# Causal convolution on sixteen 32x32 tiles, one pool of eight PSUM banks, and a first batch on the whole array

## The chip, the cores and the metric

The kernel runs on one core of one Trainium2 chip. The metric is the device time of one execution in microseconds (us). The median of 3 runs before the change was 392.44 us (391.48 to 392.64). The profile's span, from the first to the last instruction, is about 2 us shorter than the time.

A note on words. PE is the matmul engine, DVE the vector engine, ACT the scalar engine, POOL and SP two small engines that here mostly start DMAs. PSUM is the memory that matmuls write, in 8 banks. A *batch* is one of 8 inputs, a *token tile* is 128 tokens, a *group* is 8 token tiles, and each group runs in two *phases*.

## The reference, cut to what matters

```python
def _attn_ref(x, weight):                 # x (8, 4224, 192), weight (8 heads, 7 taps)
    w = softmax(weight, axis=-1)          # (cut: written out, with 1e-9 in the sum)
    x_pad = np.concatenate([zeros(B, 6, D), x], axis=1)
    # per head of 24 channels: out[s] = sum over k of w[h, k] * x_pad[s + k]
    out = np.einsum('hk,bskhg->bshg', w, x_unf)
    return out.reshape(B, S, D)

def _moe_ref(x, U, V, w_ch1, w_ch2):      # U (4224, 32), V (32, 4224), w_ch1 (192, 768), w_ch2 (768, 192)
    xt = x.transpose(0, 2, 1)
    h = xt @ U @ V                        # mixes all tokens of a batch through rank 32
    u = x + h.transpose(0, 2, 1)
    return u + np.maximum(u @ w_ch1, 0.0) @ w_ch2
```

A batch is 4224 tokens, or 33 token tiles. Call the convolution's output y. The mixer needs U times all of a batch's y before the first h of that batch can be made. All 8 batches make 264 token tiles, or 33 groups.

## The kernel before

The convolution along tokens is a matmul with a *band matrix*. The matrix has 128x128 entries per head, with seven diagonals that hold the taps. Tokens lie on the partitions. The first six outputs of a token tile also need the last six tokens of the tile before, which a second matmul with a small corner matrix (`bandp`) adds. For batches 1 to 7, a head takes two such corner matmuls, on 64 rows each, and two full ones with 408 columns. A second copy of x, `xh`, lets one of the corner matmuls run on the other half of the rows.

```python
    un_ps = ...tile_pool(name="un_ps", bufs=6, space=PSUM)   # everything but the output sums
    ch_ps = ...tile_pool(name="ch_ps", bufs=2, space=PSUM)   # W2's sums

    def load_x(b):                         # one large DMA, after a wait for y of the batch before
        if b > 1:
            nc.gpsimd.tensor_copy(out=seen[0:1], in_=y_tiles[b - 1][0:1, 0, 0:1])
        nc.gpsimd.dma_start(out=x_tiles[b][:, 1 : 1 + NT, :], in_=x[b].rearrange("(j p) d -> p j d", p=P))
        load_xh(b)                         # (cut: x_tiles and xh_tiles of batch b are those of b - 2)

    def conv_unit(b, parts, engs, halo=True):      # parts: (first tile, end tile, head)
        def half():                        # corner matmuls, on 64 rows
            st["ps"] = [bank() for _ in parts]
            for i, (a, e, h) in enumerate(parts):
                k = i if halo else 1
                src = x_tiles[b] if k else xh_tiles[b]
                rows = slice(k * C2, (k + 1) * C2)
                nc.tensor.matmul(out=st["ps"][i][:, 0 : (e - a) * GS], lhsT=bandp[rows, h, :],
                                 rhs=src[rows, a:e, h * GS : (h + 1) * GS], start=True, stop=False)
        def full():                        # the band itself, then a copy to y
            for i, (a, e, h) in enumerate(parts):
                nc.tensor.matmul(out=st["ps"][i][...], lhsT=band[:, h, :],
                                 rhs=x_tiles[b][:, a + 1 : e + 1, h * GS : (h + 1) * GS], start=False, stop=True)
                copy(engs[i], y_tiles[b][:, a:e, h * GS : (h + 1) * GS], ...)

    def tt_unit(b):                        # U times y, 33 matmuls in turn on 4 column tiles
        ...                                # then ACT swaps two halves and DVE adds them

    def h_unit(g, half_no):                # h of 4 tiles: V on two 64-row tiles; u = y + h on DVE
        ...

    def transpose(g):                      # a DMA transposes u of one group, from the SP queue
        nc.sync.dma_start_transpose(out=uT_tiles[g]..., in_=u_ring[...])

    # w1_piece: 6 matmuls of 512 columns (W1 times uT), then Relu on ACT or DVE
    # w2_piece: matmuls of 192 columns (Relu's output times W2), + u on DVE, DMA of the output

    # head: batch 0 in 3 chunks; U transposed by DVE; W1, W2 and x of batch 1 loaded behind x of batch 0
    ...
    for g in range(NG + 1):
        for k in range(2):
            # 3 W1 pieces of group g; h of group g + 2 (k = 1) and convolution of the next batch;
            # the DMA transpose of group g + 2 (k = 1); half the W2 matmuls of group g - 1
            ...
```

PE's program order is fixed. The W1 matmuls of a group wait for that group's DMA transpose, and the transpose waits for u, which DVE makes from h.

## Time and profile before

| what | value | view |
|---|---|---|
| time, median | 392.44 us | runs |
| first W1 matmul | 42.47 us | timeline |
| PE busy after that | 337.6 of 349.6 us | stage table |
| a group without convolution | 8.76 us | chain of waits |
| a group with three heads of it | 11.3 us | chain of waits |

The first lines of the page are the busy time of each engine, its share of the span and its number of instructions. The line PEclk holds one digit for each of 40 equal slices: the clock that PE was granted, in tenths, where 9 stands for 90% or more.

```profile
PE 354.3 (90%) x3582; PEld 226.0 (58%) x3582; DVE 264.0 (67%) x481; ACT 204.0 (52%) x381; POOL 25.1 (6%) x36
...
PEclk9999999999999999999999999999999999999999
```

The stage table of before, from 42.4 us to the end, has the busy time of each engine with its instructions, the granted clock, the DMA engines' busy share and GB/s:

```profile
core 0: us, PE busy (x) PEld busy (x) DVE busy (x) ACT busy (x) POOL busy (x), PEclk, DMA share, GB/s
42.40:392.00 349.60, 337.58 (x3475) 217.34 (x3475) 243.52 (x432) 187.45 (x357) 16.27 (x18) 1.00 0.75 140
```

PE is busy for 97% of this stage. So a matmul that is taken away shortens the run, and little else does.

The chain of waits of before shows what ended last, followed back. Its columns are start, duration, engine, tile and line, and the number of instructions. L333 is W1, L354 is W2, L295 is h, L238 and L249 are the convolution's corner and full matmuls.

```profile
306.28 0.50 PE un L295 x8
...
306.81 0.60 ACT rl_4402 L342
...
307.45 0.33 PE un L238
307.78 0.45 PE un L249 x2
...
312.26 0.52 PE un L238 x4
312.78 0.80 PE un L249 x4
...
317.60 0.50 PE un L295 x8
...
337.94 0.49 PE un L295 x8
...
346.70 0.49 PE un L295 x8
```

Read from one h to the next: 317.60 - 306.28 = 11.3 us with three heads of convolution, and 346.70 - 337.94 = 8.76 us with none. Two heads in one phase cost 0.52 + 0.80 = 1.3 us. A single head costs 0.78 us plus a wait of about 0.65 us for a Relu on ACT, which has to empty a PSUM bank first.

The head, as the timeline of before shows it (start, duration, engine, line, operation, tiles; in brackets the engine's idle time before and what ended it):

```profile
23.61 4.65 DVE L388 STREAM_TRANSPOSE U_sb<-U_in 128x1024 bf16<-128x1024 bf16 x1
...
32.20 1.62 PE L269 MATMUL un<-y_sb,U_sb 128*32 128x192 bf16 x33
...
42.47 5.54 PE L333 MATMUL un<-uT,W_sb 64*128 64x512 bf16 x36 [5.45 <-DMA uT<-u_ring]
```

The U sum can't start before 32.20 us, because DVE first spends 4.65 us on transposing U, and the convolution's last chunk waits behind it. PE then waits 5.45 us for the first DMA transpose. PE's longest wait for a transpose in this kernel is that first one, as the list of PE's waits says (total, times, longest):

```profile
PE un L333 <- DMA uT<-u_ring: 5.5, 1, 5.5
```

### The profile page before, as it was taken

The numbers are of one execution on the slowest core, as the hardware profiler recorded it, in microseconds if no ns is written. First come the engines' busy times: TensorE is split into PE (matmuls) and PEld (weight loads), VectorE is DVE, ScalarE is ACT, GpSimd is POOL, SyncE is SP. The second block draws the span as 40 slices with busy tenths as digits, with TensorE's granted clock in tenths as the row PEclk, the third lists the DMA queues.
The fourth block names the chain that finished last, engine by engine and source line by source line (L and its number), as shares of the span: only waits on it lengthen the run. The fifth ranks groups of instructions, "written<-read, shape, count | busy, mean of one in ns | idle before, by whom it ended". The sixth has DMA issues, their size and how long they took to land. (4 is left out here: it accounts for less than half of the span.)

```text
span 392.1 us, 8704 instructions
## 1 busy us (share of the span) xinstructions
PE 354.3 (90%) x3582; PEld 226.0 (58%) x3582; DVE 264.0 (67%) x481; ACT 204.0 (52%) x381; POOL 25.1 (6%) x36
## 2 busy tenths in 40 slices
PE   1546699999999999999999999999999999999995
PEld 1213356655666556666565666656666566676664
DVE  4375465867677666866777667766686767888863
ACT  5325476465555655556545565555546555544450
POOL 4040020020001100020002000020000000000000
PEclk9999999999999999999999999999999999999999
DMA  7979589759927994599635996499544542655533
GB/s 183 260 113 186 77 110 183 165 115 208 172 84 145 171 221 108 139 127 195 176 97 130 197 163 115 122 172 212 134 123 102 108 118 72 146 159 129 142 100 123
DMA packets 127208, 56.89 MB, mean 145 GB/s; under 512 B 88512, under 2 KB 126912, under 8 KB 127040
## 3 DMA queue, kind: packets, MB, share of 16 engines
q1 hardware_dynamic: 92208, 43.03, 48.3%
q0 software_dynamic: 34960, 13.31, 29.0%
q8 instruction: 28, 0.46, 0.5%
q14 instruction: 12, 0.10, 0.1%
HBM read 29.86 MB, written 25.95 MB: 142 GB/s over the span
## 5 line engine op out<-in xcount | busy, mean ns | idle before, releaser
L333 PE MATMUL un<-uT,W_sb 64*128 64x512 bf16 x1188 | 141.0, 380 | 5.5 <-DMA uT<-u_ring 5.5
L364 DVE TENSOR_TENSOR o<-ch,u_ring 128x384 f32<-128x384 f32 x132 | 73.2, 557 | 74.0 <-PE ch L354 73.7
L333 PEld LDWEIGHTS <-W_sb 64*128 64x128 bf16 x1188 | 53.3, 95 | 71.7 <-issue 17.8
L67 ACT ACTIVATE y_sb<-un 128x408 bf16<-128x408 f32 (+2 forms) x124 | 54.2, 501 | 31.2 <-PE un L249 27.2
L306 DVE TENSOR_TENSOR u_ring<-y_sb,un 128x384 bf16<-128x384 bf16 (+1 forms) x136 | 64.4, 537 | 3.2 <-PE un L295 0.6
L238 PEld LDWEIGHTS <-bandp 64*128 64x128 bf16 x136 | 11.2, 99 | 28.9 <-issue 22.5
L238 PE MATMUL un<-x_sb_121,bandp 64*128 64x408 bf16 (+2 forms) x48 | 14.2, 372 | 12.7 <-DVE x_sb_121 L69 5.7
L249 PEld LDWEIGHTS <-band 128*128 128x128 bf16 x136 | 10.2, 103 | 25.5 <-issue 22.4
L295 PE MATMUL un<-tt_sb,V_sb 64*128 64x192 bf16 x264 | 22.1, 249 | 1.3 <-DVE tt_sb L281 1.1
L295 PEld LDWEIGHTS <-V_sb 64*128 64x128 bf16 x264 | 15.5, 95 | 11.3 <-issue 2.1
L249 PE MATMUL un<-x_sb_121,band 128*128 128x408 bf16 (+2 forms) x72 | 17.8, 367 | 0.0
L249 PE MATMUL un<-x_sb_125,band 128*128 128x408 bf16 x64 | 15.0, 340 | 0.0
L100 POOL CAST seen<-y_sb 1x1 f32<-1x1 bf16 x6 | 1.1, 178 | 210.9 <-ACT y_sb L67 210.9
L238 PE MATMUL un<-x_sb_125,bandp 64*128 64x408 bf16 x32 | 10.6, 331 | 1.7 <-ACT rl_445 L342 0.2
L238 PE MATMUL un<-xh_126,bandp 64*128 64x408 bf16 x32 | 9.5, 331 | 2.3 <-ACT rl_444 L342 0.4
L69 DVE CAST y_sb<-un 128x288 bf16<-128x288 f32 (+1 forms) x12 | 5.1, 433 | 9.1 <-PE un L249 9.0
L281 DVE TENSOR_TENSOR tt_sb<-un,sw 128x192 bf16<-128x192 f32 x8 | 2.9, 358 | 8.7 <-ACT sw L279 8.7
L238 PE MATMUL un<-xh_122,bandp 64*128 64x408 bf16 x24 | 7.1, 330 | 1.8 <-ACT rl_1152 L342 0.2
L186 PE MATMUL un<-taps,sel 112*128 112x128 bf16 x10 | 1.2, 309 | 7.7 <-DVE taps L177 7.7
L269 PE MATMUL un<-y_sb,U_sb 128*32 128x192 bf16 x264 | 8.0, 262 | 0.0
L342 ACT ACTIVATE rl_355<-un 128x512 bf16<-128x512 f32 x6 | 3.6, 597 | 7.6 <-PE un L333 7.4
L101 POOL DMA_DIRECT2D x_sb_125<-in_x_dram x4 | 7.3, 1821 | 1.4 <-PE ch L354 1.4
(284 smaller groups left out, 602.7 us busy)
## 6 DMA issues: line engine op xcount, KB each, us to landing
out_dram<-o SPq DMA_DIRECT2D x132, 192.0 KB, 2.6
x_sb_125<-in_x_dram POOLq DMA_DIRECT2D x4, 1584.0 KB, 17.5
x_sb_121<-in_x_dram POOLq DMA_DIRECT2D x3, 1584.0 KB, 17.5
xf<-in_x_dram SPq DMA_DIRECT2D x2, 1152.0 KB, 13.0
xf<-in_x_dram SPq DMA_DIRECT2D x1, 864.0 KB, 19.7
W_sb<-in_moe_w_ch_dram POOLq DMA_DIRECT2D x3, 288.0 KB, 5.4
V_sb<-V_sb SPq DMA_DIRECT2D x3, 264.0 KB, 8.4
uT<-u_ring SPq DMA_TRANSPOSE x33, 3.7
```

Source lines behind the costliest of these rows:

```text
L67: nc.scalar.activation(out=out_ap, in_=in_ap, func=ACT.Copy)
L69: nc.vector.tensor_copy(out=out_ap, in_=in_ap)
L101: nc.gpsimd.dma_start(out=x_tiles[b][:, 1 : 1 + NT, :], in_=x[b].rearrange("(j p) d -> p j d", p=P))
L238: nc.tensor.matmul(out=st["ps"][i][:, 0 : (e - a) * GS], lhsT=bandp[rows, h, :], rhs=src[rows, a:e, h * GS : (h + 1) * GS], start=True, st ...
L249: nc.tensor.matmul(out=ps[:, 0 : (e - a) * GS], lhsT=band[:, h, :], rhs=x_tiles[b][:, a + 1 : e + 1, h * GS : (h + 1) * GS], start=False, ...
L269: nc.tensor.matmul(out=ps[q * R : (q + 1) * R, 0:D], lhsT=U_sb[:, j, :], rhs=y_tiles[b][:, j, :], start=j < 4, stop=j >= NT - 4,)
L281: nc.vector.tensor_tensor(out=tt_tiles[b][:], in0=ps[:, 0:D], in1=sw[:], op=ALU.add)
L295: nc.tensor.matmul(out=ps[i][:, k * D : (k + 1) * D], lhsT=V_sb[rows, j * P : (j + 1) * P], rhs=tt_tiles[b][rows, :], start=True, stop=True,)
L306: nc.vector.tensor_tensor(out=u_of(t0 + 2 * i + k, n), in0=in3(y_tiles[b][:, j : j + n, :]), in1=in3(ps[i][:, k * D : (k + n) * D].rearran ...
L333: nc.tensor.matmul(out=h1[a][:], lhsT=W1_sb[rows, c, ms], rhs=uT[rows, :, c, :], start=c == 0, stop=c == 2,)
L342: nc.scalar.activation(out=rl[a][:, m, :], in_=h1[a][:], func=ACT.Relu)
L364: nc.vector.tensor_tensor(out=in3(o[:]), in0=in3(ch[g][:]), in1=u_of(t0, 2), op=ALU.add)
```

## The change

The intent is to give PE fewer and cheaper convolution matmuls, to remove the waits for PSUM banks, and to start the steady state earlier.

- Batches 1 to 7: x is stored as four row quarters of 32 partitions. Blocks of 32 tokens make the band matrix 32x32, so a pair of heads takes 64 matmuls on the 16 tiles of the array, in 4 rounds. The corner matrix is just another 32x32 block, and `xh` goes.
- One rotating pool of 8 PSUM banks instead of 6 + 2.
- h on four 32-row tiles. The U sum's four partial sums are added by one matmul with a constant matrix (`add4`) that also copies the sum to all four row blocks.
- Batch 0 stays on the whole array, in 4 chunks. U is transposed on PE. V is asked for later (at 14.3 us instead of 4.2), the weights behind the third of the four chunks (at 19.6 us instead of 22.9), the U sum follows each chunk, and the first transpose of u is done on PE. Dummy matmuls (`keep_warm`) are put in the head.

```diff
-    un_ps = ...tile_pool(name="un_ps", bufs=6, space=PSUM)
-    ch_ps = ...tile_pool(name="ch_ps", bufs=2, space=PSUM)
+    banks = ...tile_pool(name="banks", bufs=8, space=PSUM)
...
     def load_x(b):
         if b > 1:
             nc.gpsimd.tensor_copy(out=seen[0:1], in_=y_tiles[b - 1][0:1, 0, 0:1])
-        nc.gpsimd.dma_start(
-            out=x_tiles[b][:, 1 : 1 + NT, :], in_=x[b].rearrange("(j p) d -> p j d", p=P)
-        )
-        load_xh(b)
+        for r in range(4):
+            n = 4 * n_of(r, NX)
+            nc.gpsimd.dma_start(
+                out=x_bufs[b % 2][32 * r : 32 * r + 32, 1 : 1 + n, :], in_=tokens(b, r, 0, n)
+            )
+        load_before(b)                     # three small DMAs of six rows
...
+    def conv_unit(b, heads):
+        ps = [bank() for _ in range(4)]
+        for i, h in enumerate(heads):      # two heads
+            for k in range(2):             # block itself, block before
+                for r in range(4):         # row tile
+                    for c in range(4):     # column tile
+                        o = ps[r][32 * c : 32 * c + 32, 0 : e * nh * GS]
+                        nc.tensor.matmul(
+                            out=o.rearrange(...)[:, :, i * GS : (i + 1) * GS],
+                            lhsT=band_of(r, h, k),            # 32 x 32
+                            rhs=x_bufs[b % 2][rows, c + 1 - k : 4 * e + c - 2 - k : 4, h * GS : (h + 1) * GS],
+                            start=k == 0, stop=k == 1,
+                        )
+        # four copies on ACT, one for each row tile's bank
...
+    def tt_sum(b, eng):
+        nc.tensor.matmul(out=ps[:, 0:D], lhsT=add4[:], rhs=tt_tiles[b][:], start=True, stop=True)
...
+    work = {2: [(1, 0)], 3: [(1, 1)], 4: [(1, 2), (1, 3)]}     # phase: (batch, unit)
...
+            for i, (b, u) in enumerate(work.get(p, [])):
+                conv_unit(b, [2 * u, 2 * u + 1])
+                if u == 0 and b + 1 < B:
+                    load_x(b + 1)
             if k and g + 2 < NG:
-                units = [h_unit(g + 2, 0), h_unit(g + 2, 1)] + units
+                h_unit(g + 2)
+                transpose(g + 2)
```

## The prediction

> **What bounds the kernel now.** TensorE: in the stage table PE is busy 337.6 of the 349.6 us after 42.4 us, DVE 243.5, ACT 187.5. The chain of waits is almost all PE, with a few waits of 0.6 us for an ACT Relu that frees a PSUM bank.
>
> Sums read from that chain and the timeline:
> - A group of 8 token tiles without convolution takes 8.76 us (two W1 pieces of 2.05, two W2 pieces of about 2.09, h 0.50): 33 x 8.76 = 289 us.
> - A group with 3 heads of convolution takes 11.3 us. A single head in an odd phase waits about 0.65 us for a bank. Per batch 6.8 us, plus 0.95 for the U sum (33 matmuls in 0.85): 7 x 7.75 = 54 us.
> - Head: the first W1 matmul starts at 42.47 us. Batch 0's x has landed at 22.4, but a DVE transpose of U (4.65 us, until 28.3) delays the last cast, the U sum starts at 32.2, and PE waits 5.45 us for the first DMA transpose. Tail about 5 us.
>
> **What the change does, costed.**
> 1. Convolution of batches 1 to 7: per pair of heads 64 matmuls of 32x32 with 192 or 216 columns, in 4 rounds of 16 tiles. If tiles overlap fully, a round takes about 92 ns (the U sum, on 4 column tiles, starts four matmuls within 8 ns and the next four 82 ns later, for 192 columns): 0.37 us a unit. If PE can't issue faster than the 20.3 ns per load+matmul pair that this trace shows, 1.3 us. The Trainium skill (TensorE: Matmul & The Clock Gate, Part 3) gives 10.6x for 16 tiles. I take 0.75 us plus 0.15 for changing the tiling: 28 x 0.9 = 25 us, instead of 47.
> 2. With 8 rotating banks I find no bank wait over 0.3 us; the 0.65 us waits go (counted in 1).
> 3. h on four row tiles: 0.50 to about 0.30 us: -6 us.
> 4. The U sum gains an fp32 128x128 matmul and two ACT copies: about +0.5 us each, +3 us.
> 5. Head: U transposed on PE, x in four chunks, V and weights later, U sum by chunk, first transpose on PE: first W1 at about 27.5 us, -15. Given back: group 1's DMA transpose (about 1 us) and batch 1's x (about 12 us of packets after the weights, landing about 36.5, needed about 35): +2.5.
>
> ACT and DVE work is nearly unchanged (DVE about 7.7 us per group, so close to binding in groups without convolution).
>
> **Sum.** 27.5 + 2.5 + 33 x 8.56 + 25 + 10 + 5 = about 353 us; I say 354, 80% range 341 to 371. Nearly all of it is on the critical path, since PE is. Faster by over 2%: 94%; within 2%: 4%; slower: 2%.
>
> **What would show it.** First W1 near 27.5 us in the timeline; a convolution unit of 64 matmuls spanning 0.5 to 1.3 us; h 0.3 us; groups with one unit about 9.5 us, without 8.55; no Relu waits before convolution; about 1650 more PE matmuls.
>
> **What would make it wrong.** PE issue slower than 20 ns per pair (unit 1.6 to 2 us: convolution gains nothing, total about 380); the four copies per unit arriving together on ACT and holding Relus and so banks; DVE becoming the limit (groups over 9 us); batch 1's x landing past 42 us and stalling PE, whose program order puts that convolution first; slow weight loads on small tiles; the head's ACT and DVE work longer than I added up.

## More of the kernel before

A transpose is issued about one group ahead of its use.

The view of the tile uT, which holds the transposes' results, ends with the time from issue to landing:

```profile
DMA to landing us min/median/max: 3.6/3.7/9.9
```

So some transposes of before landed after 8 to 10 us instead of 3.7. Nobody on PE waited for them.

## The result, and the profile after

The changed kernel took 369.88 us (median of 4 runs, 368.55 to 371.23) against 392.54 us beside it. The result is correct. The ratio is 0.943, with a 95% interval of 0.939 to 0.947. A ratio here is the mean time of one kernel's fast runs over that of the other's in the same rounds, so it is not quite the ratio of the medians.

The page of after, the same lines:

```profile
PE 342.8 (93%) x5248; PEld 223.8 (61%) x5250; DVE 253.2 (69%) x474; ACT 197.9 (54%) x382; POOL 40.1 (11%) x72
...
PEclk9577898999899999999999999999999999999999
```

There are 1666 more matmuls, and PE is still busy less. The clock line now dips in the head, and again in slices 7 and 11, which are about 55 to 64 us and 92 to 101 us.

The stage table of after, from its first W1 matmul:

```profile
core 0: us, PE busy (x) PEld busy (x) DVE busy (x) ACT busy (x) POOL busy (x), PEclk, DMA share, GB/s
36.10:366.00 329.90, 316.83 (x5057) 209.20 (x5056) 238.35 (x429) 185.16 (x357) 29.44 (x49) 0.98 0.80 151
```

The chain of waits of after. L377 is W1, L398 W2, L328 h, L263 the convolution:

```profile
170.50 0.28 PE bank L328 x8
...
174.91 0.73 PE bank L263 x55
175.64 2.09 PE bank L398 x24
177.72 2.05 PE bank L377 x18
179.77 0.28 PE bank L328 x8
...
190.35 0.31 PE bank L328 x8
...
192.63 10.18 DMA uT<-u_ring
...
202.85 2.12 PE bank L377 x18
204.97 0.72 PE bank L263 x55
...
306.64 0.28 PE bank L328 x8
...
315.19 0.28 PE bank L328 x8
```

A group with two heads takes 179.77 - 170.50 = 9.27 us, and a unit of convolution 0.73 us. Groups without convolution take 315.19 - 306.64 = 8.55 us. No Relu stands in these groups any more. Four of 0.4 us or more are left in the chain: three on ACT before W2 matmuls near 50 and 99.5 us, and one on DVE before a convolution unit at 125.4 us, just behind a late transpose. In their place is something that before did not have: a DMA transpose that takes 10.18 us, and that W1 waits for. The list of PE's waits has six of them, and one wait of 2.1 us for no semaphore at all:

```profile
PE bank L377 <- DMA uT<-u_ring: 7.9, 6, 2.8
...
PE bank L398 <- issue: 2.1, 1, 2.1
```

The timeline of after shows the first W1 matmul, both stalls, and what stood beside them:

```profile
36.12 5.57 PE L377 MATMUL bank<-uT,W_sb 64*128 64x512 bf16 x36
...
57.22 0.34 PE L398 MATMUL bank<-W_sb,rl_533 128*128 128x192 bf16 x2
59.68 0.64 PE L398 MATMUL bank<-W_sb,rl_533 128*128 128x192 bf16 x3 [2.13 <-issue]
...
186.14 3.18 POOL L111 DMA_DIRECT2D x_sb_85<-in_x_dram  x4 [0.39 <-PE bank L398]
...
192.63 3.34 SPq L349 DMA_TRANSPOSE uT<-u_ring  x1
...
202.85 1.47 PE L377 MATMUL bank<-uT,W_sb 64*128 64x512 bf16 x12 [0.87 <-DMA uT<-u_ring]
```

The load of a batch's x is issued at 186.14 us and its last part lands at 202.63 us, by its records. The transpose issued in between, at 192.63 us, lands at 202.81 us. The last line of the tile uT's view:

```profile
DMA to landing us min/median/max: 3.6/4.1/12.2
```

An account of the span, which fell by 24.6 us (392.1 to 367.5). The first W1 matmul came 6.35 us earlier. PE's busy time after it fell by 20.8 us. PE's idle time after it, the tail after the last matmul included, rose by 2.5 us (12.1 to 14.6). In before no idle stretch after the first W1 matmul was longer than 0.3 us by PE's records. In after there are seven, of 10.0 us together. They are 1.1 us at 42.0, 2.1 at 57.6, 2.9 at 87.5, and four of 0.8 to 1.2 us, about one for each load of x.

Two readings needed tests. Is the gain really that of the tiles, or of the pool? And what took back what the forecast had promised?

### The profile page after: what moved, and what is told of

It is laid out like the page before. It is cut to its first block, busy times and chain, and to the rows that moved or that the text cites. A ratio compares the mean times of both kernels' runs of the same rounds, so it can differ in the third digit from the quotient of the medians.

```text
span 367.5 us, 12088 instructions
## 1 busy us (share of the span) xinstructions
PE 342.8 (93%) x5248; PEld 223.8 (61%) x5250; DVE 253.2 (69%) x474; ACT 197.9 (54%) x382; POOL 40.1 (11%) x72
## 4 chain that ended last, share of the span: by engine, by line
PE 73%; DMA 19%; DVE 3%; issue 2%; ACT 2%; DVEq 0%
PE bank L377 30%; PE bank L398 29%; DMA uT<-u_ring 16%; PE bank L263 4%; DMA xf<-in_x_dram 3%; PE bank L287 2%; DVE u_ring L339 2%; PE bank L328 2%; PE bank L300 2%; PE bank L316 1%; PE bank L425 1%; ACT x_sb_85 L65 1%; PE bank L360 1%; DVE y_sb L67 0%; ACT y_sb L65 0%
## 5 line engine op out<-in xcount | busy, mean ns | idle before, releaser
L377 PE MATMUL bank<-uT,W_sb 64*128 64x512 bf16 x1188 | 142.7, 384 | 8.0 <-DMA uT<-u_ring 7.9
L408 DVE TENSOR_TENSOR o<-bank,u_ring 128x384 f32<-128x384 f32 x132 | 70.8, 553 | 68.4 <-PE bank L398 58.5
L377 PEld LDWEIGHTS <-W_sb 64*128 64x128 bf16 x1188 | 53.7, 95 | 76.1 <-issue 13.5
L339 DVE TENSOR_TENSOR u_ring<-y_sb,bank 128x384 bf16<-128x384 bf16 (+1 forms) x136 | 64.5, 537 | 11.1 <-PE bank L328 11.1
L65 ACT ACTIVATE y_sb<-bank 128x432 bf16<-128x432 f32 (+5 forms) x122 | 51.3, 502 | 8.3 <-PE bank L287 6.5
L263 PEld LDWEIGHTS <-band 32*32 32x32 bf16 x1568 | 15.6, 88 | 13.3 <-issue 11.9
L328 PE MATMUL bank<-tt_sb,V_sb 32*128 32x192 bf16 x264 | 12.4, 252 | 0.9 <-ACT tt_sb L65 0.4
L328 PEld LDWEIGHTS <-V_sb 32*128 32x128 bf16 x264 | 4.3, 93 | 14.2 <-issue 13.9
L111 POOL DMA_DIRECT2D x_sb_86<-in_x_dram x16 | 12.6, 797 | 1.7 <-PE bank L398 1.4
L263 PE MATMUL bank<-x_sb_86,band 32*32 32x192 bf16 (+1 forms) x896 | 12.4, 251 | 0.1
L204 PE MATMUL bank<-warm 128*128 128x512 bf16 x23 | 8.9, 523 | 1.3 <-DVE warm L139 1.2
L111 POOL DMA_DIRECT2D x_sb_85<-in_x_dram x12 | 9.5, 802 | 1.3 <-PE bank L398 1.0
L263 PE MATMUL bank<-x_sb_85,band 32*32 32x192 bf16 (+1 forms) x672 | 9.1, 251 | 0.0
L287 PE MATMUL bank<-x_sb_85,bandp 128*128 128x288 bf16 (+3 forms) x32 | 8.8, 321 | 0.0
L263 PE MATMUL bank<-x_sb_86,bandp 32*32 32x192 bf16 x128 | 8.5, 244 | 0.0
```

The costliest lines, as they stand in the source:

```text
L65: nc.scalar.activation(out=out_ap, in_=in_ap, func=ACT.Copy)
L111: nc.gpsimd.dma_start(out=x_bufs[b % 2][32 * r : 32 * r + 32, 1 : 1 + n, :], in_=tokens(b, r, 0, n))
L204: nc.tensor.matmul(out=ps[:], lhsT=warm[:, 0:P], rhs=warm[:], start=True, stop=True)
L263: nc.tensor.matmul(out=o.rearrange("p (t g) -> p t g", g=nh * GS)[:, :, i * GS : (i + 1) * GS], lhsT=band_of(r, h, k), rhs=x_bufs[b % 2][r ...
L287: nc.tensor.matmul(out=ps[:, :, (h - i) * GS : (h - i + 1) * GS], lhsT=(bandp if k else band)[:, h, :], rhs=x_bufs[0][:, a + 1 - k : e + 1 ...
L328: nc.tensor.matmul(out=ps[r][:, k * D : (k + 1) * D], lhsT=V_sb[rows, j * P : (j + 1) * P], rhs=tt_tiles[b][rows, :], start=True, stop=True,)
```

## The experiments

Theory A: the tiles and the pool each shorten PE's work. What was given back is the contention of the x loads with the DMA transposes, and a head bound by DMA. Rivals: the tiles are worth little and the pool everything; PE stalls come from issuing or from bank waits; the head is bound by the slow clock.

The experiments ran on three chips. The kernel before ran beside each of them, with medians of 392.2 to 393.3 us, so about 1 us of a difference between runs on two chips can be the chip's. Each ratio is to before in the same rounds.

### e1: convolution on the whole array again

All else is as in after. A pair of heads takes 8 matmuls of 128 rows in place of 64 small ones, and x is loaded by one DMA.

```diff
-        for r in range(4):                 # four quarter loads and load_before
-            ...
+        nc.gpsimd.dma_start(out=x_bufs[b % 2][:, 1 : 1 + NT, :], in_=x[b].rearrange("(j p) d -> p j d", p=P))
...
+        for h in heads:
+            for a, e in ((0, 17), (17, NT)):
+                ps = bank()[:, 0 : (e - a) * GS]
+                for k in range(2):
+                    nc.tensor.matmul(..., lhsT=(bandp if k else band)[:, h, :],
+                        rhs=x_bufs[b % 2][:, a + 1 - k : e + 1 - k, ...], start=k == 0, stop=k == 1)
```

> Undoes the small tiles alone: batches 1 to 7 convolve on the whole array as batch 0 does (8 matmuls of 408 columns per pair of heads, x loaded in the old layout). Theory (the tiles save PE time): a unit takes about 1.38 us instead of 0.73, a group with one unit 9.9 us instead of 9.27, so 28 x 0.65 = +18 us of PE work over the changed kernel; part is given back because longer groups leave the DMA transposes more slack (up to 8 us of waits in the trace) and fewer instructions run short (up to 4 us): +6 to +18 us, about 376 to 388. Rival (the gain of the change is the bank pool and the head, the tiles are worth nothing): within 2 us of 369.9.

Measured: 380.46 us (378.67 to 380.65), ratio 0.968 (0.963 to 0.973), correct. So without the tiles the kernel is 10.6 us slower. Its chain of waits around one unit:

```profile
287.10 0.28 PE bank L318 x8
...
291.51 1.45 PE bank L255 x8
292.96 1.98 PE bank L388 x24
...
296.99 0.28 PE bank L318 x8
```

L318 is h in this kernel. The unit takes 1.45 us instead of 0.73, and the W2 matmuls behind it show 0.11 us less. Whole groups say it best, from one h to the next: 296.99 - 287.10 = 9.89 us against 9.27. That is 0.62 us for each of 28 units, or 17 us (an estimate from these two group times). The total moved by only 10.6 us. In the tiled kernel some 7 us of that were paid elsewhere: e1's first W1 came 0.9 us earlier (35.2), its PE gaps over 0.3 us sum to 8.4 us against 10.0, and it has neither of the two stretches of half clock that after has behind its long gaps (3.4 us long each, so about 3.4 us of delay together, an estimate). 17.4 - 0.9 - 1.6 - 3.4 = 11.5 us, close to what the total shows. The rival (tiles worth nothing) is refuted.

### e2: x of batches 2 to 7 never loaded

This kernel is wrong on purpose (relative error 1.15): the buffers keep old data. It asks what the loads cost.

```diff
-                if u == 0 and b + 1 < B:
+                if u == 0 and b + 1 < 2:
                     load_x(b + 1)
```

> Wrong result on purpose: x of batches 2 to 7 is never loaded, the convolutions read what the buffers hold. All else is the same. Theory (the waits before W1 come from DMA transposes that are queued beside the load of the next batch's x): the transposes at 78, 113, 153, 193 and 232 us land in 3.7 to 5 us instead of 10 to 12, the PE gaps of 3.1, 1.45, 1.3, 1.1 and 1.1 us before W1 go, and the slow clock window at 90 us with them: 8 to 10 us faster, about 360 to 362. Rival (those waits come from the DVE adds or from banks, which feed the transposes late): less than 2 us faster, gaps stay.

Measured: 357.28 us (355.51 to 357.46), ratio 0.909 (0.904 to 0.914). It is 12.6 us faster than after. The last line of the tile uT's view in e2:

```profile
DMA to landing us min/median/max: 3.6/3.7/5.0
```

Every transpose lands in time, and after 44 us no PE gap is over 0.5 us. The 2.1 us gap at 57 us is gone as well, though two units of convolution stand in the same phase as in after. So the loads cost about 12 us, more than I had expected, and nearly all that PE lost in after's steady state goes with them. The amount of arithmetic is the same.

### e3: the whole load of x, later

If the trouble is that the load is issued just before a transpose, issue it just after one.

```diff
-                    load_x(b + 1)                   # in the phase of the batch's first unit
+                    pending.append(b + 1)           # batches 3 to 7
...
                 transpose(g + 2)
+                if pending:                         # waits for u of the group just transposed
+                    load_x(pending.pop(), gate=u_of(t - 1, 2)[0:1, 1, 0, 0:1])
```

> The same loads, but x of batches 3 to 7 is asked for when the input of the next transpose is written, about 6 us later, so that this transpose goes ahead of the load. Theory (a transpose that is issued while a load is under way lands only when the load is through, about 17 us after the load's issue; what matters is the place of the load between two transposes): transposes take at most 8 us, no PE gap over 0.5 us before W1 from group 7 on, 6 to 10 us faster than 369.9. Rival (the DMA engines' total load is the limit, wherever the load stands): the waits move to the next transpose, within 2 us.

Measured: 374.35 us (372.11 to 376.72), ratio 0.954 (0.947 to 0.960), correct. This is a miss. It is 4.5 us slower than after, not faster. PE's waits in e3:

```profile
PE bank L380 <- DMA uT<-u_ring: 10.6, 6, 2.8
```

The waits moved to the next transpose, and grew. In this kernel the load takes 20 to 22 us from its issue to its last landing, and transposes come every 9.3 us. Wherever a load of this size starts, a transpose falls into it. The rival for this run was right that the waits move. Its size was not: it said within 2 us, and its cause, the total load of the DMA engines wherever it stands, does not fit e6, which moves the same bytes and is faster.

### e4: one unit of convolution for each phase in batch 1

This tests whether the stall at 57 us comes from the two units (128 small matmuls) in one phase.

```diff
-    work = {2: [(1, 0)], 3: [(1, 1)], 4: [(1, 2), (1, 3)]}
+    work = {1: [(1, 0)], 2: [(1, 1)], 3: [(1, 2)], 4: [(1, 3)]}
```

> The four convolution units of batch 1 stand one to a phase (1, 2, 3, 4) instead of two in phase 4. Theory (256 convolution instructions in a row outrun the fetch of PE's instructions: the 2.4 us gap at 57.3 us is in the middle of an accumulation, without a semaphore, and a 16 KB instruction fetch starts at that moment; the half clock window after it costs up to 1.7 us more): the gap goes, 2 to 5 us faster than 369.9. Rival (the gap is a chance of one profile, or the work only moves): within 1 us.

Measured: 369.73 us (366.01 to 372.15), ratio 0.939 (0.930 to 0.947), correct; the profiled run, the longest of the four, was slow. The total did not move, so as a saving it is a miss. In its profile the stall did not go. It moved to 53 us, into a unit of convolution, and is 1.5 us long there, with no semaphore; since that run was slow, this is an indication and not a size. In after, PE fetches instructions in blocks of 16 KB, and the record of one begins at 57.27 us, 0.05 us after the last matmul before the stall started. PE has 41 such fetches in after and 28 in before. (That these fetches are PE's is read from their number alone.) With e2, where no load stood beside it and the stall was absent, this points to an instruction fetch that is delayed by a load of x. The pointer is weak: the record of that fetch ends at 58.2 us, 1.5 us before PE goes on, and in e3 the same stall (57.53 to 60.17 us) begins 0.2 us before the nearest fetch. No run isolates it.

### e5: pools of 6 and 2 banks again

```diff
-    banks = ...tile_pool(name="banks", bufs=8, space=PSUM)
+    banks = ...tile_pool(name="banks", bufs=6, space=PSUM)
+    ch_ps = ...tile_pool(name="ch_ps", bufs=2, space=PSUM)
```

> Undoes the bank pool alone: 6 rotating banks and 2 for the W2 sums, as in the kernel before; the tiles stay. Theory A (the common pool is what removed the Relu waits): a convolution unit needs 4 banks right after W1 has used 6, so it waits for the Relus of the middle W1 piece, and h likewise; about 0.3 to 0.6 us for each of 28 units and 31 h, +10 us or more. Theory B (the waits went because the convolution now stands only in even phases, away from h, with one unit in a group): within 3 us of the changed kernel's 369.9.

Measured: 378.88 us (378.37 to 380.40), ratio 0.964 (0.961 to 0.967), correct. It is 9 us slower, so the pool is worth about as much as the tiles. That is Theory A, a little under its 10 us. Its chain of waits:

```profile
290.53 0.86 PE bank L264 x53
...
295.53 0.48 PE bank L329 x8
```

Here h takes 0.48 us, about as in before, although it stands on four row tiles. The convolution unit takes 0.86 us. So without the pool the row tiles gain nothing for h; I had credited the gain to them. The cause is in the start times of h's matmuls. In after, the first four start within 0.01 us. In e5, at 295.46 us, the third starts 0.10 us after the first and the fourth 0.23 us after it, each 0.05 us behind the end of a Relu (on ACT at 295.51, on DVE at 295.64) that empties the bank it needs. An earlier matmul still runs meanwhile, so PE is not idle and the list of waits shows nothing. The four starts of before have such steps too, behind the Relus that end at 306.27 and 306.40 us: there the last of the eight matmuls starts 0.41 us after the first, where rounds of 0.082 us would give 0.25. So on two row tiles without these waits h would take about 0.33 us (an estimate from these starts), and of the 0.22 us that h gained, the four row tiles account for about 0.05 and the pool for the rest. No run has two row tiles with the pool. The two durations also give the total: 28 x 0.13 + 31 x 0.20 = 9.8 us, against the 9.0 measured.

### e6 and e6b: x in quarters, each behind its own transpose

A quarter load is a quarter of the bytes, so it should be through before the next transpose.

```diff
-    def load_x(b):
+    def load_x(b, parts=range(4), gate=None):
...
+    loads = {0: [(2, 0)], 1: [(2, 1)], 2: [(2, 2), (2, 3)], 3: [(3, 0), (3, 1)], 4: [(3, 2), (3, 3)]}
+    for b in range(4, B):
+        for r in range(4):
+            loads[(b * NT) // G - 11 + r] = [(b, r)]
...
                 transpose(g + 2)
+                if g in loads:             # waits for u of the group just transposed
+                    load_x(loads[g][0][0], [r for _, r in loads[g]], u_of(t - 1, 2)[0:1, 1, 0, 0:1])
```

Batch 2's units move to phases 8 to 11.

> The same bytes of x, but each batch's load is cut into its four row quarters and one quarter is asked for after each group's transpose, instead of four at once (batch 2's convolution is moved to phases 8 to 11). Theory (a whole load takes 17 to 21 us, more than the 9.3 us between transposes, so one transpose and some instruction fetches always stand behind it, wherever it starts; a quarter of it is through in about 5 us): every transpose from group 7 on lands in under 7 us, no PE gap over 0.5 us after 70 us, 8 to 12 us faster than 369.9, close to the 357.3 of the run without these loads. Rival (the DMA engines' total load is too high for the shorter groups): 0 to 4 us faster.

> e6 again, on the same chip as e9, as its yardstick: 362 to 364 us.

Measured: e6 362.96 us (362.08 to 363.40), ratio 0.922 (0.920 to 0.925), correct. The repeat e6b, on another chip, took 365.33 us (362.12 to 366.23), ratio 0.930 (0.926 to 0.935), and missed its own 362 to 364. That is 5 to 7 us faster than after, where I had expected 8 to 12. The slowest transpose now lands after 7.8 us. It did not work quite as I had thought: a quarter takes 7 to 10 us to land and overlaps the transpose it follows, so most transposes beside quarters land after 5.5 to 7.8 us instead of 3.7. But W1 wants them about 9.3 us after their issue, so none of these delays reaches PE. PE's waits in e6:

```profile
PE bank L262 <- DMA x_sb<-in_x_dram: 2.1, 2, 1.6
PE bank L376 <- DMA uT<-u_ring: 1.4, 1, 1.4
```

The one wait left for a transpose is that of group 1, in the head. No other W1 waits. What is left are two waits for batch 2's x itself, which now comes too late.

### e7: more dummy matmuls in the head

```diff
-    keep_warm(12)
+    keep_warm(24)
...
-    keep_warm(4)
+    keep_warm(20)
...
-            keep_warm(3)
+            keep_warm(5)
...
+    keep_warm(2)        # and 2, 3 behind the U sum and h
```

> More dummy matmuls in the head alone (24 and 20 instead of 12 and 4, 5 instead of 3 between chunks, 7 more before h and the transposes), so that TensorE's clock stays at full from about 5 us. Theory (batch 0's matmuls ran at half clock, 240 ns instead of 120 for 288 columns, but after that the head is bound by DMA: V's third copy lands at 32.5 us, x of batch 1 at 42.4, and group 1's transpose behind it at 43.0): chunk 0 takes 2 us less, the first W1 starts 1 to 2 us earlier, group 1's W1 still at about 43 us, total within 2 us of 369.9. Rival (the half clock is what made the head late): total 5 us or more faster.

Measured: 370.11 us (369.41 to 372.98), ratio 0.943 (0.938 to 0.947), correct: no change. The clock was at full speed from 6.6 us through the rest of the head, but for 3.4 us from 20.2 us; in after it was half from 8.5 to 18.7 us, from 22.1 to 25.6 and from 32.4 to 39.2. Batch 0's first matmuls of 288 columns came every 120 ns instead of every 240. The timeline of e7:

```profile
35.14 4.06 PE L377 MATMUL bank<-uT,W_sb 64*128 64x512 bf16 x36 [0.30 <-ACT uT L65]
...
42.23 2.12 PE L377 MATMUL bank<-uT,W_sb 64*128 64x512 bf16 x18 [2.65 <-DMA uT<-u_ring]
```

The first W1 came 1.0 us earlier. PE then waited 2.65 us for group 1's transpose, which landed at 42.19, 0.8 us earlier than in after. Between first W1 and landing stands x of batch 1, which landed at 41.4 us. So the start of group 1 is bound by DMAs, as I had expected of this run, and not by the clock. Before that, V's last copy, which landed at 31.8 us, held h for 0.7 us.

### e8: the head and the quarters together

e6 and e7, V asked for earlier, group 1's transpose on PE too, and batch 1's convolution one phase later.

```diff
+    V_sb = cst.tile([P, S], BF16, name="V_sb")            # moved up, behind U's load
+    nc.gpsimd.dma_start(out=V_sb[0:R, :], in_=moe_V[:])
...
-    transpose(1)
+    transpose_pe(1)
...
-    work = {2: [(1, 0)], 3: [(1, 1)], 4: [(1, 2), (1, 3)]}
+    work = {3: [(1, 0), (1, 1)], 4: [(1, 2), (1, 3)]}
```

> The quarters of e6 and the dummy matmuls of e7, and in the head V asked for at 2 us, group 1's transpose on PE instead of DMA, and batch 1's convolution in phases 3, 3, 4, 4 instead of 2, 3, 4, 4. Theory: the first W1 starts at about 31 us, group 1's W1 directly after group 0's at about 36, and batch 1's x (42 us) is needed only then; 4 to 6 us faster than e6, about 353 to 357. Rival (DMA in the head takes back what is saved): within 2 us of e6.

Measured: 365.19 us (363.70 to 365.35), ratio 0.928 (0.925 to 0.930), correct. A miss: no better than e6. The first W1 came at 35.3 us, not at 31, because group 1's transpose on PE now stands before it. Group 1's W1 started 3.4 us earlier than in after (39.6 us), but there were gaps on PE of 1.9 us at 48.0, of 0.9 and 1.8 us at 77 to 78, and of 1.2 us at 98.4. That of 1.8 us is a wait for batch 2's x, that of 0.9 us one for an output sum on DVE, and the other two (3.1 us) wait for no semaphore. The earlier head was paid back in waits; that all of them are due to the loads is not shown.

### e9: loads and units spread further, a failure

It was e6 with e8's early V and dummy matmuls, with group 1's transpose on PE behind the first W1 pieces, and with later phases for batches 2 and 3.

```diff
-    transpose(1)                                          # e6's
...
+                if p == 0:                                # behind the first W1 pieces
+                    transpose_pe(1)
...
-        phases = ... else [8, 9, 10, 11]
+        phases = {2: [9, 10, 11, 12], 3: [13, 14, 16, 18]}.get(b, ...)
```

> From e8, with three placements changed that its trace showed to cost: group 1's transpose on PE stands after the first half of group 0's W1 instead of before it (1.7 us), batch 1's convolution is back in phases 2, 3, 4, 4, and batch 2's and 3's convolutions start one phase later (9 to 12, and 13, 14, 16, 18), since their x landed 2 us late. Theory: first W1 at about 33.5 us, group 1's W1 at about 39, no wait for x at 77 us; a gap of an instruction fetch may stay where units stand beside a load; 3 to 7 us faster than e6, about 356 to 360. Rival (fetches and loads take it back again): within 2 us of e6.

Measured: a wrong result (relative error 0.129), 367.11 us (363.87 to 368.55), ratio 0.938 (0.935 to 0.940). The mistake is mine. Batch 4 shares a buffer with batch 2, and its first quarter was asked for before batch 2's last unit, in program order, had read the buffer. The order that I wrote was kept; it was the wrong one. I draw nothing from its time. It is told because moving loads earlier has this edge.

### e10: the same with batch 4's quarters one step later

```diff
+    loads[8] = [(4, 2), (4, 3)]
+    loads[7] = [(4, 1)]
+    loads[6] = [(4, 0)]
+    del loads[5]
```

> e9 with its mistake mended: there the first quarter of batch 4's x was asked for one phase before batch 2's last convolution unit, so that unit read batch 4 (the wrong result) and waited 7.4 us for the load, with a slow clock window after it. Here batch 4's quarters follow groups 6, 7, 8 and 8. Theory: that wait and its window go, nothing else changes: correct, 362.1 - 7.4 - 1.7 to 3.4 us of span, about 352 to 356 us. Rival (the loads only move the wait elsewhere): 360 us or more.

Measured in 6 runs, of which the longest (363.11 us) was slow: 359.37 us (357.58 to 363.11), ratio 0.917 (0.913 to 0.920), correct. It is 33 us faster than before and 10.5 us faster than after, and has the lowest time of all correct versions; the intervals of its ratio and of e6's just touch. It missed its own forecast of 352 to 356 us. The first W1 came at 33.2 us, group 1's at 38.5. PE's waits in e10 no longer name a transpose. Its longest wait after the head is:

```profile
PE bank L264 <- DMA x_sb<-in_x_dram: 1.8, 1, 1.8
```

That is batch 4's x, at 133 us, and 3.4 us of half clock followed from 137.5 us. Otherwise no PE gap after the first W1 is over 0.3 us.

## Why the prediction was right or wrong

The direction and the bound were right, and the time lay at the upper edge of the range: 369.9 us, with 354 predicted and 341 to 371 given. The forecast saved 38 us, and 22.7 came. Term by term, from the profile of after:

| term | predicted, us | measured, us |
|---|---|---|
| first W1 matmul | 27.5 | 36.1 |
| PE waits given back | 2.5 | 10.0 (seven gaps over 0.3) |
| 33 groups | 33 x 8.56 = 282.5 | 33 x 8.55 = 282.2 |
| 28 convolution units | 28 x 0.90 = 25.2 | 28 x 0.73 = 20.4 |
| 7 U sums | 10 | 7 x (10.58 - 9.27) = 9.2 |
| tail | 5 | 3.8 |
| half clock after the first W1 | none | about 4.9, an estimate |
| small gaps | none | 0.8 |
| sum | 352.7 | 367.4, of a span of 367.5 |

The estimate of the half clock is half of each stretch that the clock record shows after the first W1 matmul: (3.1 + 3.4 + 3.4) / 2. The group with a U sum takes 10.58 us in the chain of waits.

**Right.** PE bounds the kernel, and removed PE time shortens it. The tiles overlap: a unit took 0.73 us, where I took 0.75 and 0.15 on top for changing the tiling, which never showed. The groups take 9.27 and 8.55 us, where I wrote 9.5 and 8.55. The Relu waits before convolution are gone but for the one at 125.4 us, and 1666 matmuls were added, where I wrote 1650. DVE did not become the limit. The total owes something to luck: the units came 4.8 us cheaper than I had allowed, and without that the time (about 375 us, an estimate) would have lain above my range.

**Right in part by luck.** h fell to 0.28 us, as predicted, but I credited four row tiles. With 6 + 2 banks the same h takes 0.48 us (e5). By the starts of its matmuls most of the gain is the pool's (about 0.17 of 0.22 us, an estimate), and I had counted the pool only in the convolution.

**Mis-sized: "first W1 at about 27.5 us, -15".** It came at 36.1 us, 8.6 us late, so the head gained 6.35 us. I had added up compute and taken full clock. The granted clock was half in much of batch 0's convolution, which doubled its matmuls (240 ns for 288 columns, 120 in e7). Taking that away gained 1.0 us for the first W1 and nothing in the total (e7). V's last copy landed at 32.6 us, and h needs all four copies, but that held half of h's matmuls by only 0.25 us (32.35 to 32.60) in after. In e10, with V there by 25.9 us and the clock at full, the first W1 still came at 33.2 us, 5.7 us after my forecast. So clock and V together explain at most 2.9 us. In after the chain of waits names no DMA between the landing of the first chunk (13.5 us) and the first W1: it is casts, PE's matmuls and copies of the four chunks. Most of this miss is thus a chain of compute that I had added up too short; which of its links is open.

**Mis-sized: "Given back: ... +2.5".** I had priced group 1's transpose and batch 1's load, and stopped there. That part measured 1.1 us (the gap at 42.0). Taking the loads of batches 2 to 7 away gives 12.6 us (e2). In before, the same delays existed, with landings after 8.3 to 9.9 us, but W1 wanted these transposes 13.0 us after their issue, so 3.4 to 4.7 us were to spare. In after W1 wants them 9.35 us after their issue (the landings less the waits), and the five beside loads that it waits for land after 10.1 to 12.2 us. So the change itself used up the slack, and the landings grew a little as well. Cutting the load into quarters removes the waits (e6). Moving it whole does not (e3). Of the dangers that I had named, slow issue, slow weight loads and DVE as the limit did not occur, and a late Relu on ACT held h only twice, for 0.2 us each. Two came partly true: batch 1's x landed past 42 us, but it delayed a transpose and not the convolution, and the head's work was longer than I had added up.

**Not settled.** The stall of 2.1 us without a semaphore is gone without the loads of x (e2), and an instruction fetch begins next to it, which is a correlation. Which long gaps are followed by half clock is open too, as the last section says. The gains of tiles, pool and quarters were each measured against after alone; how they add is not known.

## What to carry to other kernels

When you shorten the busy engine's work, look at what lands with the least slack in the old trace: the outliers of a DMA's landing time are the next wait, even if nobody waits for them yet. Cut a large load into pieces, each of which delays an urgent small transfer by less than its slack; moving it whole only chooses which transfer is hit. And predict a head link by link, with the landing times of its loads, its casts and copies, and the clock that it will get.

## What the Trainium skill lacked or had wrong

- *DMA: Bandwidth & Descriptors*, section "Queues, rings and completion order", says that each DMA engine takes turns between the queue rows that have work, a packet at a time. It gives no figure for a DMA transpose beside a bulk load on another queue. Here such transposes landed after 10.1 to 12.2 us instead of 3.7, ending about with the load (192.63 to 202.81 us; load's end 202.63).
- *TensorE: Matmul & The Clock Gate*, section "Why this matters for your kernels", advises against PE idle gaps over about 3 us. Here gaps of 2.1 and 2.9 us (after), 1.6 us (e6) and 1.8 us (e10), as PE's records show them, were followed by about 3.4 us of half clock, while gaps of 1.9 us in e1, 2.3 us in e5 and even 2.8 us in e3 (at 215.6 us) were not. The length of 3.4 us agrees with the window of about 3.4 us that the page gives in its section "What's actually happening". In these traces half clock followed shorter gaps than the rule suggests, and a gap's length alone does not decide.
- The same page, section "Wait — 56ns, not 53.3ns?", says that matmuls never start less than about 25 ns apart. On different tiles they do: in one unit of after (at 174.9 us) the first 16 started about 3.3 ns apart, and the last 32 about 8.3 ns. The page's Part 3, with about 4 ns between tiles, is the nearer of the two. Its 10.6x for 16 tiles, which the prediction cites, is not what a band matrix gains over a whole array with all its rows in use: 0.73 us for the 64 small matmuls against 1.45 us for the 8 whole ones, or 2x (after against e1).
- *Runtime: NRT & Kernel Launch*, section "Instruction fetch mechanics", calls the cost of a fetch of 16 KiB mostly hidden. Here one began within 0.3 us of a stall of 2.1 us, beside a load of x; that it is the cause is not shown, and no run isolates it.
- No page of those that I read says that waits for a PSUM bank can hide inside the busy time of a group of matmuls, where one matmul still runs while the next waits: h took 0.48 us with 6 + 2 banks and 0.28 us with 8 (e5 against after), with no wait over 0.4 us in total in the list of PE's waits for it.
